# A fused attention and FFN kernel on one core: all 3,359 operations of its hand-kept order put at new places

## The chip, the core and the metric

The kernel runs on one core of one Trainium2 chip. Its engines are TensorE (PE, with PEld for its weight loads), VectorE (DVE), ScalarE (ACT), GpSimd (POOL) and SyncE (SP), and 16 DMA engines move data. The metric is the device time of one launch, in microseconds.

## What is computed

The first half is attention in which a query sees only the keys whose nearest centroid is its own. The second half is a feed-forward layer with the activation h * tanh(softplus(h)), called mish below. The core of the reference:

```python
q_assign = np.argmax(np.einsum('bhsd,hcd->bhsc', q_n, c_n), axis=-1)
k_assign = np.argmax(np.einsum('bhsd,hcd->bhsc', k_n, c_n), axis=-1)
mask = q_assign[:, :, :, None] == k_assign[:, :, None, :]
scores = scale * np.matmul(q, k.transpose(0, 1, 3, 2))
scores = np.where(mask, scores, -1000000000.0)
attn = softmax(scores)                      # over the last axis, with 1e-9 in the divisor
x = np.matmul(attn, v)                      # 4 batches, 8 heads, 768 rows, 64 columns each
h = x.reshape(3072, 512) @ w_in             # 512 x 2048
out = (h * np.tanh(softplus(h))) @ w_out    # 2048 x 512
```

## The kernel before

Attention has 32 groups (batch and head, number n), each with three blocks of 256 queries. Such a block is a unit i, 96 in all, and it has two halves a of 128 queries. For one half the steps are these:

- `scores` (L646, L651): four matmuls fill a tile s in PSUM. Two such tiles exist, and the assignment tiles use the same two.
- `rowmax` (L663, DVE), then `expo` (L677, ACT), which reads s, writes the probabilities p and sets the tile s free. There are three buffers p.
- `total` and `recip` (small DVE operations), `p_hi` (L715, POOL) and `p_lo` (L732, DVE). They split p into a high and a low half-precision part, in a tile hl of which there are three. `p_lo` sets p free.
- `ptrans` (L748): a transposing DMA on SP's queue from hl into the tile pt.
- `pv` (L768): for a pair of units m, 36 matmuls that use 64 of the array's columns each. `pv_out` (ACT) and `x_lo` (DVE) put the result into x.

The first 24 units go another way: transposes on PE (L725), full-precision `pv`. Before a group can be scored its operands A, B, T and Z are made: `prep_hi` and `prep_lo` on POOL, then `copy_t` (T from A), `copy_z`, `copy_b` (B from T), `copy_a` and `hot_copy`, mostly DMAs. Those at L529 are issued by SP or by ACT, and L636 and L637 by SP. `v_load` and `v_sq` bring the values in by SP and square them on ACT (L383).

The feed-forward layer has matmuls `m1` (h, L847 to L849), the activation `e_mish` (L858, ACT), `e_gh` (POOL) and `e_gl` (L872, DVE), and matmuls `m2` (O, L984 to L986). Its result goes out by `m_out` (L992, ACT) and `m_store` (L998, SP). The last part is done with seven block products instead of eight (`n_mul`, `k_mul`).

ACT changes its table between exponential and mish; each change is a row ACT_TABLE_LOAD.

The order of all this is written out: the string `ORDER` has one entry per operation, `RANK` gives its place, and `Plan.run` emits the operations sorted by it. `Plan.tie` makes each engine run its instructions in the order in which they were emitted, and gives the buffers out in that order. So the string sets, for each engine and each DMA queue, what stands behind what.

Of the kernel before, what the change touches and what calls it, by code (L numbers as in the profile page):

```python
# [1568 lines left out]
w_low 1, scores 0 1, rowmax 0 0, rowmax 0 1, w_f32 3, copy_z 1, w_abs 2, hot_copy 1, expo 0 0, expo 0 1, w_abs 0, p_hi
0 1, w_low 0, p_hi 0 0, scores 1 0, p_lo 0 0, scores 1 1, p_lo 0 1, scores 2 0, rowmax 1 0, w_f32 2, v_max 0, rowmax 1  # L1570
1, w_f32 1, w_f32 0, rowmax 2 0, ptrans 0 0, expo 1 0, ptrans 0 1, expo 1 1, p_hi 1 1, p_hi 1 0, p_lo 1 0, scores 2 1,
v_cross 0, p_lo 1 1, ptrans 1 0, copy_b 1, rowmax 2 1, v_peak 0, ptrans 1 1, expo 2 0, w_low 7, prep_hi 2, w_low 6,
prep_lo 2, total 0 1, w_low 17, total 1 1, w_low 5, w_low 4, p_hi 2 0, w_abs 7, expo 2 1, p_hi 2 1, w_sq 0, pv 0 0,
p_lo 2 0, scores 3 0, v_wide 0, scores 3 1, pv 0 1, w_f32 7, recip 0 1, rowmax 3 0, recip 1 1, rowmax 3 1, copy_t 2,
w_load 9, w_load 8, copy_z 2, qk_load 4, hot_copy 2, copy_a 2, w_load 15, copy_b 2, w_load 12, pv 0 2, p_lo 2 1,
scores 4 0, ptrans 2 0, w_abs 5, w_abs 6, w_abs 4, expo 3 0, expo 3 1, ptrans 2 1, p_hi 3 1, p_hi 3 0, p_lo 3 0,
scores 4 1, w_sq 1, p_lo 3 1, scores 5 0, w_f32 6, w_f32 4, v_scale 0, rowmax 4 0, pv_out 0, pv_out 1, rowmax 4 1,
x_lo 0, x_lo 1, ptrans 3 0, expo 4 0, ptrans 3 1, expo 4 1, p_hi 4 1, p_hi 4 0, w_sq 2, p_lo 4 0, w_low 8, w_low 16,
total 3 1, total 4 1, total 2 1, prep_hi 3, prep_lo 3, w_low 9, recip 3 1, rowmax 5 0, recip 4 1, recip 2 1, w_f32 5,
total 1 0, w_abs 8, ptrans 4 0, w_abs 9, expo 5 0, total 0 0, recip 0 0, recip 1 0, scores 5 1, p_lo 4 1, pv 1 0, pv 1  # L1580
1, p_hi 5 0, pv 1 2, w_sq 3, p_lo 5 0, scores 6 0, w_f32 8, rowmax 5 1, ptrans 4 1, w_abs 17, w_f32 17, expo 5 1,
pv_out 2, p_hi 5 1, total 5 1, w_abs 12, recip 5 1, w_abs 16, ptrans 5 0, w_low 12, w_low 10, pv_out 3, w_low 15,
rowmax 6 0, expo 6 0, x_lo 3, scores 6 1, w_sq 4, w_sq 5, w_sq 6, w_sq 7, p_lo 5 1, scores 7 1, w_f32 9, rowmax 6 1,
ptrans 5 1, w_f32 12, rowmax 7 1, expo 6 1, x_lo 2, p_hi 6 1, p_hi 6 0, p_lo 6 0, scores 7 0, pv 2 0, qk_load 5,
qk_load 7, w_load 14, w_load 13, w_load 21, qk_load 6, copy_z 3, copy_t 3, hot_copy 3, w_load 20, copy_b 3, copy_a 3,
w_load 18, w_load 22, w_load 19, v_load 1 0, total 3 0, rowmax 7 0, w_abs 11, w_abs 10, w_abs 14, w_abs 15, w_abs 13,
expo 7 0, ptrans 6 0, expo 7 1, p_hi 7 1, recip 3 0, total 4 0, recip 4 0, total 2 0, recip 2 0, pv 2 1, pv 2 2, w_low
11, w_low 14, w_low 13, total 6 1, total 7 1, w_f32 11, w_f32 14, recip 6 1, w_f32 10, w_f32 13, w_f32 15, w_f32 16,
w_low 21, pv_out 4, p_hi 7 0, assign_mm 1, p_lo 6 1, scores 8 0, w_sq 8, w_sq 9, p_lo 7 0, scores 8 1, w_sq 10, w_sq
11, w_sq 12, p_lo 7 1, w_sq 13, w_sq 14, total 5 0, x_lo 4, assign_turn 1, rowmax 8 0, assign_max 1, recip 7 1, rowmax  # L1590
8 1, ptrans 6 1, w_abs 21, ptrans 7 0, expo 8 0, prep_hi 4, w_f32 21, ptrans 7 1, w_sq 15, expo 8 1, total 8 1, pv_out
5, w_sum 0, p_hi 8 0, p_lo 8 0, scores 9 0, w_spread 0, pv 3 0, p_hi 8 1, assign_hot 1, rowmax 9 0, assign_back 1, pv
3 1, pv 3 2, assign_put 1, scores 9 1, recip 5 0, w_scale 0, recip 8 1, assign_stg 1, rowmax 9 1, w_abs 20, ptrans 8
0, expo 9 0, w_abs 18, pv_out 6, pv_out 7, x_lo 6, x_lo 7, p_hi 9 0, p_lo 8 1, scores 10 0, w_sq 16, p_lo 9 0, ptrans
8 1, expo 9 1, ptrans 9 0, w_low 20, w_low 22, prep_lo 4, w_low 19, w_low 18, w_hi 0, p_hi 9 1, w_f32 18, rowmax 10 0,
w_lo 0, scores 10 1, p_lo 9 1, ptrans 9 1, rowmax 10 1, expo 10 0, expo 10 1, w_abs 19, total 6 0, recip 6 0, w_sq 17,
pv 4 0, total 9 1, w_hi 1, recip 9 1, w_f32 20, w_lo 1, p_hi 10 1, p_hi 10 0, p_lo 10 0, scores 11 0, pv 4 1, pv 4 2,
copy_t 4, copy_a 4, copy_z 4, hot_copy 4, w_load 25, copy_b 4, w_load 26, w_load 23, total 9 0, recip 9 0, scores 11
1, p_lo 10 1, total 10 1, w_hi 2, prep_hi 5, ptrans 10 0, w_abs 22, rowmax 11 0, w_f32 19, recip 10 1, pv_out 8, expo
11 0, pv_out 9, rowmax 11 1, w_lo 2, ptrans 10 1, x_lo 8, x_lo 9, total 7 0, recip 7 0, p_hi 11 0, expo 11 1, p_hi 11  # L1600
1, prep_lo 5, w_hi 3, total 11 1, scores 12 0, w_sq 18, w_sq 19, w_sq 20, p_lo 11 0, scores 12 1, p_lo 11 1, w_sq 21,
scores 13 0, ptrans 11 0, rowmax 12 0, expo 12 0, rowmax 12 1, ptrans 11 1, w_abs 23, expo 12 1, w_abs 26, w_lo 3,
w_f32 22, recip 11 1, rowmax 13 0, total 8 0, recip 8 0, copy_t 5, v_load 1 2, v_load 1 3, copy_z 5, w_load 24,
qk_load 8, copy_b 5, hot_copy 5, copy_a 5, qk_load 9, w_load 29, w_load 27, w_load 28, w_load 30, p_hi 12 1, w_hi 4,
p_hi 12 0, pv 5 0, p_lo 12 0, scores 13 1, p_lo 12 1, pv 5 1, pv 5 2, w_lo 4, rowmax 13 1, ptrans 12 0, w_abs 25, expo
13 0, ptrans 12 1, expo 13 1, w_hi 5, total 12 1, w_lo 5, w_low 23, pv_out 10, w_low 25, recip 12 1, pv_out 11, w_low
26, w_low 24, total 13 1, prep_hi 6, x_lo 11, p_hi 13 0, p_lo 13 0, w_sq 22, scores 14 0, scores 14 1, p_hi 13 1, x_lo
5, total 10 0, recip 10 0, p_lo 13 1, ptrans 13 0, w_f32 23, rowmax 14 0, rowmax 14 1, ptrans 13 1, w_abs 24, expo 14
0, expo 14 1, v_sq 1 0, p_hi 14 0, w_sq 23, pv 6 0, pv 6 1, p_lo 14 0, scores 15 0, scores 15 1, w_hi 6, w_low 27,
prep_lo 6, total 14 1, w_low 28, w_low 30, w_low 29, p_hi 14 1, w_f32 25, w_f32 26, recip 13 1, w_f32 24, rowmax 15 0,  # L1610
rowmax 15 1, w_lo 6, moe_scale_h 0, p_lo 14 1, pv 6 2, total 11 0, recip 11 0, ptrans 14 0, v_sq 1 2, ptrans 14 1,
expo 15 0, pv_out 12, expo 15 1, pv_out 13, p_hi 15 0, w_sq 24, p_lo 15 0, scores 16 0, w_sq 25, ptrans 15 0, w_abs
27, p_hi 15 1, total 12 0, recip 12 0, x_lo 10, x_lo 13, p_lo 15 1, scores 16 1, rowmax 16 0, ptrans 15 1, w_f32 27,
rowmax 16 1, recip 14 1, total 15 1, expo 16 0, w_abs 28, w_abs 29, expo 16 1, p_hi 16 0, pv 7 0, w_sq 26, w_sq 27,
p_lo 16 0, scores 17 0, p_hi 16 1, copy_t 6, copy_z 6, w_load 31, hot_copy 6, copy_a 6, copy_b 6, qk_load 10, v_load 1
1, total 16 1, w_low 31, prep_hi 7, recip 15 1, w_f32 28, w_f32 29, rowmax 17 0, total 15 0, recip 15 0, scores 17 1,
pv 7 1, pv 7 2, w_sq 28, w_sq 29, p_lo 16 1, w_abs 30, ptrans 16 0, expo 17 0, w_abs 31, w_f32 30, rowmax 17 1, w_f32
31, expo 17 1, pv_out 14, ptrans 16 1, total 17 1, pv_out 15, prep_lo 7, w_hi 7, x_lo 15, x_lo 14, p_hi 17 1, p_hi 17
# [295 lines left out]
```

## Time and profile before

| | us |
|---|---|
| three timed runs | 860.67, 857.17, 860.91; median 860.67 |
| the profiled execution | 856.9, of which the span of its instructions 855.2 |
| PE busy | 833.8 (97%) |
| DVE, ACT, POOL busy | 675.7 (79%), 544.1 (64%), 433.6 (51%) |
| DMA | mean 143 GB/s, 122.50 MB |

Busy time counts an engine as busy from an instruction's start to its end; matmuls are pipelined and their ends are modelled. The difference between the span and the execution's time lies before the first and behind the last instruction.

### The profile page before, as it was taken

How to read it: one execution, taken by the hardware profiler on the slowest of the kernel's cores; microseconds unless marked ns; L12 is line 12 of the kernel's file. 1: busy time of each engine (PE TensorE's matmuls, PEld its weight loads, DVE VectorE, ACT ScalarE, POOL GpSimd, SP SyncE). 2: the span in 40 equal slices, each digit the busy share in tenths (PEclk: the TensorE clock that was granted, in tenths of full speed). 3: DMA queues.
4: the chain of work that ended last, by engine and by line, in shares of the span. 5: the costliest groups of instructions: out<-in, count | busy, mean ns of one | idle time of the engine just before them, and what ended most of it. 6: DMA issues, size and time to landing. Idle time of an engine off the chain costs nothing.

```text
span 855.2 us, 17553 instructions
## 1 busy us (share of the span) xinstructions
PE 833.8 (97%) x6743; PEld 622.9 (73%) x6743; DVE 675.7 (79%) x1192; ACT 544.1 (64%) x925; POOL 433.6 (51%) x417
## 2 busy tenths in 40 slices
...
GB/s 339 298 247 185 213 135 43 114 192 163 176 200 154 174 181 122 148 163 116 173 153 174 190 171 127 150 177 162 136 146 146 148 112 96 15 1 2 2 8 80
DMA packets 253460, 122.50 MB, mean 143 GB/s; under 512 B 230368, under 2 KB 230880, under 8 KB 253376
## 3 DMA queue, kind: packets, MB, share of 16 engines
...
## 4 chain that ended last, share of the span: by engine, by line
PE 52%; DVE 4%; DMA 3%; ACT 2%; POOL 1%; issue 1%; ACTq 0%; SPq 0%; POOLq 0%; DVEq 0%
PE h L847 7%; PE h L849 6%; PE h L848 6%; PE o L768 5%; PE O L984 5%; PE O L985 5%; PE O L986 5%; PE s L646 3%; PE s L651 3%; DMA pt<-hl 2%; PE cn L937 2%; DVE hl L732 1%; PE cy('k', 1)_10960 L1131 1%; PE cy('k', 0)_10720 L1131 1%; DVE m L663 1%
## 5 line engine op out<-in xcount | busy, mean ns | idle before, releaser
L677 ACT ACTIVATE p<-s,m 128x768 f32<-128x768 f32 x192 | 173.0, 902 | 120.4 <-DVE m L663 59.1
L715 POOL TENSOR_SCALAR hl<-p,l 128x768 f16<-128x768 f32 x144 | 157.3, 1095 | 168.2 <-DVE l L697 92.5
L663 DVE TENSOR_REDUCE m<-s 128x1 f32<-128x768 f32 x192 | 179.8, 949 | 29.5 <-PE s L651 27.1
L732 DVE SCALAR_TENSOR_TENSOR hl<-p,l,hl 128x768 f16<-128x768 f32 x144 | 165.7, 1159 | 30.2 <-POOL hl L715 30.0
L847 PE MATMUL h<-x,w 128*128 128x256 f16 x640 | 175.2, 274 | 0.0
L849 PE MATMUL h<-x,w 128*128 128x256 f16 x640 | 174.5, 273 | 0.0
L848 PE MATMUL h<-x,w 128*128 128x256 f16 x640 | 174.4, 273 | 0.0
L646 PE MATMUL s<-A,B 128*128 128x384 f32 x384 | 117.0, 385 | 11.8 <-ACT p L677 10.0
L984 PE MATMUL O<-w,g 128*128 128x512 f16 x288 | 109.8, 381 | 0.0
L986 PE MATMUL O<-w,g 128*128 128x512 f16 x288 | 109.2, 379 | 0.0
L985 PE MATMUL O<-w,g 128*128 128x512 f16 x288 | 109.2, 379 | 0.0
L651 PE MATMUL s<-Z,T 80*128 80x384 f32 x384 | 99.2, 339 | 0.4 <-DVE T L618 0.4
L847 PEld LDWEIGHTS <-w 128*128 128x128 f16 x768 | 75.1, 98 | 24.4 <-issue 13.2
L864 POOL TENSOR_SCALAR g<-u,mscg 128x512 f16<-128x512 f32 x72 | 70.8, 987 | 43.5 <-ACT u L858 24.9
L848 PEld LDWEIGHTS <-w 128*128 128x128 f16 x768 | 75.3, 98 | 11.3
L646 PEld LDWEIGHTS s<-A,B 128*128 128x128 f32 x384 | 62.0, 190 | 29.2 <-ACT p L677 17.1
L849 PEld LDWEIGHTS <-w 128*128 128x128 f16 x768 | 75.1, 98 | 8.7
L858 ACT ACTIVATE u<-h,msch 128x512 f32<-128x512 f32 x80 | 53.8, 687 | 43.1 <-PE h L849 28.8
L768 PE MATMUL o<-pt,v 128*64 128x256 f16 x1296 | 78.1, 274 | 0.8 <-DMA pt<-hl 0.8
L768 PEld LDWEIGHTS <-v 128*64 128x64 f16 x1296 | 68.1, 110 | 11.8 <-issue 11.3
L872 DVE SCALAR_TENSOR_TENSOR g<-u,mscg,g 128x512 f16<-128x512 f32 x72 | 69.0, 964 | 5.9 <-POOL g L864 5.8
L651 PEld LDWEIGHTS s<-Z,T 80*128 80x128 f32 x384 | 69.9, 189 | 0.7 <-ACT w L285 0.7
(241 smaller groups left out, 1393.2 us busy)
## 6 DMA issues: line engine op xcount, KB each, us to landing
...
```

Source lines behind the costliest of these rows:

```text
L646: nc.tensor.matmul(s[:, j, :384], st["B", n][:, q0 : q0 + P], st["A", n][:, j * 384 : (j + 1) * 384], start=True, stop=False,)
L651: nc.tensor.matmul(s[:, j, :384], st["T", n][: D + NCL, q0 : q0 + P], st["Z", n][: D + NCL, j * 384 : (j + 1) * 384], start=False, stop=True,)
L663: nc.vector.tensor_reduce(m, st["s", i, a][:, :, :384], axis=AX.XY, op=ALU.max, negate=True)
L677: nc.scalar.activation(p.rearrange("p (n x) -> p n x", n=2), st["s", i, a][:, :, :384], AF.Exp, bias=st["m", i, a], scale=1.0, accum_out=l,)
L715: nc.gpsimd.tensor_scalar(t[:, 0], p, r, 1.0, op0=ALU.mult, op1=ALU.mult)
L732: nc.vector.scalar_tensor_tensor(t[:, 1], p, r, t[:, 0], op0=ALU.mult, op1=ALU.subtract)
L768: nc.tensor.matmul(o[s * D : s * D + D, :256], v if early else v[:, int(part == 1)], st["pt", 2 * m + s][:, :, c + (0 if early or part < 2 ...
L847: nc.tensor.matmul(o, wh, xh, start=(c == 0), stop=False)
L848: nc.tensor.matmul(o, wh, xl, start=False, stop=False)
L849: nc.tensor.matmul(o, wl, xh, start=False, stop=(c == 3))
L984: nc.tensor.matmul(o, gh, wh, start=(f == 0 and fi == 0), stop=False)
L985: nc.tensor.matmul(o, gh, wl, start=False, stop=False)
```

## The change

Every operation keeps its work, its engine and its buffers; only the string `ORDER` is another. The diff replaces all 317 lines of it. Two pairs of lines show what it looks like:

```diff
-21 1, pv 21 2, e_mish 20, e_mish 21, copy_t 16, pv_out 42, pv_out 43, m1 23 0, scores 46 0, m1 23 1, scores 47 0, m2 2
-16, ptrans 45 0, ptrans 45 1, expo 46 1, copy_b 16, copy_a 16, expo 46 0, rowmax 47 0, expo 47 0, copy_t 17, e_mish
...
+16, p_hi 44 0, e_gh 18, expo 45 0, copy_t 16, expo 45 1, m_out 1 1, e_mish 20, assign_put 4, scores 47 0, pv 21 0,
+ptrans 45 0, ptrans 45 1, copy_b 16, expo 47 0, expo 46 1, copy_a 16, expo 46 0, e_mish 22, total 46 1, recip 46 1,
```

Most operations stay within a few places of where they stood. PE has as many matmuls as before. ACT loses four table loads, 96 before and 92 now.

**First place: ACT, the copies of group 16.** This is ACT's order around the middle of the program, with the DMA that copies T from A at the top and the one that copies B from T below it. Names are out<-in, and p46_1 is the tile p of unit 46, half 1. Before:

```order
L529 DMA T_16_4351<-A_16_4243 64x768
L805 ACTIVATE x1_3_0_4353<-o21_4297 64x256
L805 ACTIVATE x1_3_1_4355<-o21_4297 64x256
L677 ACTIVATE p46_1_4465,l46_1_4466<-s46_1_4292,m46_1_4318 128x768
L529 DMA B_16_4246<-T_16_4351 64x768
L527 CAST A_16_4243<-A_16_4243 64x768
L677 ACTIVATE p46_0_4470,l46_0_4471<-s46_0_4370,m46_0_4450 128x768
L677 ACTIVATE p47_0_4475,l47_0_4476<-s47_0_4387,m47_0_4473 128x768
```

ACT's order with the change, from the same copy of T to the first exponential behind the copy of B:

```order
L529 DMA T_16_4270<-A_16_4259 64x768
L677 ACTIVATE p45_1_4272,l45_1_4273<-s45_1_4131,m45_1_4254 128x768
L992 ACTIVATE osb1_1_4275<-O1_1_3951,msco0_2275 128x512
L857 ACT_TABLE_LOAD
L858 ACTIVATE u20_4278<-h20_4193,msch0_1834 128x512
L805 ACTIVATE x1_3_0_4348<-o21_4289 64x256
L805 ACTIVATE x1_3_1_4350<-o21_4289 64x256
L858 ACTIVATE u21_4352<-h21_4230,msch0_1834 128x512
L860 ACT_TABLE_LOAD
L383 ACTIVATE vq2_0_4355,vm2_3782<-vraw2_0_4183 128x768
L529 DMA B_16_4262<-T_16_4270 64x768
L677 ACTIVATE p47_0_4466,l47_0_4467<-s47_0_4284,m47_0_4447 128x768
```

Three operations stood between the two copies, and nine stand there now.

**Second place: ACT, the squares of the last batch's values.** vq3_1 is the square of the tile vraw3_1, which a DMA on SP's queue loads. ACT before, from the copy of B of group 23:

```order
L529 DMA B_23_6402<-T_23_6549 64x768
L858 ACTIVATE u43_6616<-h43_6521,msch1_3891 128x512
L860 ACT_TABLE_LOAD
L383 ACTIVATE vq3_1_6752,vm3_6751<-vraw3_1_6743 128x768
L805 ACTIVATE x2_2_1_6234<-o32_6637 64x256
L805 ACTIVATE x2_2_2_6556<-o32_6637 64x256
L677 ACTIVATE p68_0_6756,l68_0_6757<-s68_0_6516,m68_0_6625 128x768
```

ACT with the change, from the same copy of B:

```order
L529 DMA B_23_6404<-T_23_6555 64x768
L677 ACTIVATE p68_0_6755,l68_0_6756<-s68_0_6512,m68_0_6624 128x768
L805 ACTIVATE x2_2_1_6226<-o32_6640 64x256
L805 ACTIVATE x2_2_2_6557<-o32_6640 64x256
L383 ACTIVATE vq3_0_6761,vm3_6760<-vraw3_0_6593 128x768
L677 ACTIVATE p69_0_6799,l69_0_6800<-s69_0_6689,m69_0_6769 128x768
```

The exponential of unit 68 now stands ahead of the square, and it is another tile's square. Among the rows of SP's queue the load of vraw3_1 moved from 259 to 248, that of vraw3_0 from 241 to 250, that of vraw3_3 from 224 to 245 and that of vraw3_2 from 263 to 269.

**Third place: SP, the store of osb2_0.** This is SP's queue of DMAs; osb2_0 is written by ACT's `m_out`. Before:

```order
L489 DMA qk23_4707<-in_qk_dram 128x768
L636 DMA Z_17_4704<-stg4_4444 16x768
L637 DMA T_17_4478<-stg4_4444 16x768
L748 DMA_TRANSPOSE pt48_4950<-hl48_0_4694 128x12x128
L748 DMA_TRANSPOSE pt48_4950<-hl48_1_4696 128x12x128
L748 DMA_TRANSPOSE pt49_4953<-hl49_1_4904 128x12x128
L998 DMA out_0_dram<-osb2_0_4761 128x512
```

SP with the change, at the same stretch:

```order
L636 DMA Z_17_4679<-stg4_4306 16x768
L637 DMA T_17_4653<-stg4_4306 16x768
L529 DMA A_17_4441<-A_17_4441 64x768
L489 DMA qk23_4684<-in_qk_dram 128x768
L998 DMA out_0_dram<-osb2_0_4775 128x512
L748 DMA_TRANSPOSE pt48_4969<-hl48_1_4671 128x12x128
```

The store stood behind three transposes of units 48 and 49; now it stands ahead of them, and on ACT `m_out` of osb2_0 stands seven rows behind the exponential of unit 48, half 1.

## Rows read from the trace of the kernel before

**Rows 1.** The page: the span, and PE's and other engines' busy time.

```profile
span 855.2 us, 17553 instructions
...
PE 833.8 (97%) x6743; PEld 622.9 (73%) x6743; DVE 675.7 (79%) x1192; ACT 544.1 (64%) x925; POOL 433.6 (51%) x417
```

**Rows 2.** Busy time by stretch: its length, each engine's busy us, clock, DMA.

```profile
20.00:200.00 180.00, 173.67 (x1426) 135.53 (x1428) 164.05 (x275) 143.32 (x295) 127.51 (x132) 0.99 0.72 181
200.00:700.00 500.00, 491.69 (x3935) 355.23 (x3932) 396.47 (x688) 323.67 (x506) 287.12 (x259) 1.00 0.83 156
700.00:840.00 140.00, 140.00 (x1207) 115.06 (x1206) 96.05 (x184) 61.54 (x99) 14.92 (x16) 1.00 0.12 26
```

**Rows 3.** PE's groups in 200 to 700 us: count, busy, mean ns, idle before.

```profile
L646 PE MATMUL s<-A,B 128*128 128x384 f32 x252 | 77.7, 389 | 6.5 <-ACT p L677 5.6 <-issue 0.9
```

**Rows 4.** Timeline at 310 to 321 us, ACT and PE: start, length, idle before.

```profile
310.79 0.47 ACTq L529 DMA_DIRECT2D T<-A  x1
317.84 0.47 ACTq L529 DMA_DIRECT2D B<-T  x1
318.35 0.83 ACT L527 CAST A<-A 64x768 fp32r<-64x768 f32 x1 [3.69 <-issue]
320.25 0.62 PE L646 MATMUL s<-A,B 128*128 128x384 f32 x2 [0.90 <-ACT p L677]
```

**Rows 5.** Timeline at 486 to 497 us, SP, ACT and PE.

```profile
486.83 1.78 SPq L371 DMA_DIRECT2D vraw<-in_vP_dram  x1
493.65 0.84 ACT L383 ACTIVATE vq<-vraw 128x768 bf16<-128x768 f32 x1 [3.25 <-DMA vraw<-in_vP_dram]
496.44 0.61 PE L646 MATMUL s<-A,B 128*128 128x384 f32 x2 [1.20 <-ACT p L677]
```

**Rows 6.** Timeline at 350 to 353 us, ACT and PE.

```profile
350.31 1.28 ACT L677 ACT_TABLE_LOAD   x1 [1.37 <-DVE hl L732]
351.60 0.90 ACT L677 ACTIVATE p<-s,m 128x768 f32<-128x768 f32 x1
352.65 0.61 PE L646 MATMUL s<-A,B 128*128 128x384 f32 x2 [0.71 <-ACT p L677]
```

**Rows 7.** Timeline at 652 to 661 us, SP and PE.

```profile
652.34 1.44 SPq L748 DMA_TRANSPOSE pt<-hl  x1
656.37 0.59 SPq L529 DMA_DIRECT2D A<-A  x1
660.33 0.58 PE L646 MATMUL s<-A,B 128*128 128x384 f32 x2 [0.86 <-issue]
```

**Rows 8.** Timeline at 324 to 327 us, PE: a `pv` between two kinds.

```profile
324.04 0.52 PE L651 MATMUL s<-Z,T 80*128 80x384 f32 x2
324.49 2.16 PE L768 MATMUL o<-pt,v 128*64 128x256 f16 x36
326.58 0.39 PE L984 MATMUL O<-w,g 128*128 128x512 f16 x1
```

**Rows 9.** PE at 31 us and at 137 to 142 us, and the clock there.

```profile
30.91 1.95 PE L768 MATMUL o<-pt,vraw 128*64 128x256 f32 x16
137.16 0.62 PE L646 MATMUL s<-A,B 128*128 128x384 f32 x2 [1.55 <-ACT p L677]
138.16 3.51 PE L768 MATMUL o<-pt,vraw 128*64 128x256 f32 x16
138.00:140.00 2.00, 2.00 (x12) 1.17 (x12) 2.00 (x3) 0.00 (x0) 0.55 (x1) 0.59 0.04 6
```

**Rows 10.** Groups over the whole span: count, busy us, mean ns, idle.

```profile
L677 ACT ACTIVATE p<-s,m 128x768 f32<-128x768 f32 x192 | 173.0, 902 | 120.4 <-DVE m L663 59.1 <-DVE hl L732 25.7 <-DVE l L689 12.5
L992 ACT ACTIVATE osb<-O,msco 128x512 f32<-128x512 f32 x18 | 12.4, 686 | 15.9 <-PE O L986 15.7
L732 DVE SCALAR_TENSOR_TENSOR hl<-p,l,hl 128x768 f16<-128x768 f32 x144 | 165.7, 1159 | 30.2 <-POOL hl L715 30.0
L715 POOL TENSOR_SCALAR hl<-p,l 128x768 f16<-128x768 f32 x144 | 157.3, 1095 | 168.2 <-DVE l L697 92.5 <-DMA pt<-hl 33.2 <-issue 11.8
```

**Rows 11.** DMA issues: count, median us from issue to landing.

```profile
pt<-hl SPq DMA_TRANSPOSE x144, 4.1
```

More of the change, by code (lines that the diff above doesn't have):

```diff
@@ L1569 @@
[L1569 to L1618, printed above, removed]
@@ L1769 @@
-m1 44 0, m1 44 1, scores 70 0, m_out 4 1, copy_t 24, v_sq 3 2, expo 69 1, pv_out 66, pv_out 67, copy_a 24, e_mish 44,
-v_sq 3 0, p_lo 69 0, e_gl 42, total 69 1, x_lo 66, x_lo 67, p_lo 68 1, p_lo 68 0, e_gl 43, rowmax 70 0, recip 69 1, m1
-45 1, scores 70 1, m2 5 0 0, m1 47 0, scores 71 0, assign_put 6, m2 5 0 1, m2 5 0 2, m1 47 1, scores 71 1, e_gh 44,
-p_hi 69 1, rowmax 70 1, p_lo 69 1, rowmax 71 0, moe_scale_h 2, assign_stg 6, ptrans 69 0, copy_z 24, m_store 4 1,
-ptrans 68 1, ptrans 68 0, ptrans 69 1, hot_copy 24, expo 70 0, copy_b 24, expo 70 1, expo 71 0, v_sq 3 3, e_mish 45,
@@ new lines @@
+15 0, w_abs 27, rowmax 16 0, w_f32 27, rowmax 16 1, ptrans 15 1, recip 15 1, recip 14 1, w_abs 30, expo 16 0, w_abs
+29, expo 16 1, w_abs 28, p_hi 16 0, pv 7 0, w_sq 26, w_sq 27, p_lo 16 0, scores 17 0, scores 17 1, pv 7 1, p_hi 16 1,
+copy_t 6, copy_z 6, hot_copy 6, w_load 31, copy_b 6, copy_a 6, qk_load 11, v_load 1 3, w_low 30, w_low 28, prep_hi 7,
+w_low 29, w_low 31, w_f32 30, rowmax 17 0, rowmax 17 1, w_f32 28, w_f32 29, total 15 0, recip 15 0, pv 7 2, w_sq 28,
+p_lo 16 1, ptrans 16 0, expo 17 0, expo 17 1, w_abs 31, w_f32 31, pv_out 14, ptrans 16 1, total 16 1, total 17 1,
@@ new lines @@
+prep_lo 7, pv_out 15, w_hi 7, x_lo 15, x_lo 14, p_hi 17 1, p_hi 17 0, w_sq 29, w_sq 30, w_sq 31, w_sum 1, p_lo 17 0,
+scores 18 0, ptrans 17 0, total 13 0, recip 13 0, p_lo 17 1, scores 18 1, rowmax 18 0, recip 16 1, recip 17 1, ptrans
+17 1, expo 18 0, pv 8 0, w_spread 1, rowmax 18 1, w_scale 1, w_lo 7, p_hi 18 0, p_lo 18 0, expo 18 1, ptrans 18 0,
+p_hi 18 1, scores 19 0, scores 19 1, p_lo 18 1, pv 8 1, w_hi 8, total 18 1, rowmax 19 0, rowmax 19 1, w_lo 8, pv 8 2,
+v_sq 1 3, ptrans 18 1, expo 19 0, expo 19 1, copy_z 7, copy_t 7, qk_load 10, v_load 1 1, hot_copy 7, copy_b 7, copy_a
@@ new lines @@
+ptrans 39 0, pv_out 36, pv_out 37, expo 41 0, expo 40 1, expo 40 0, v_sq 2 1, copy_b 14, copy_a 14, x_lo 36, total 41
+0, x_lo 37, total 40 0, total 40 1, recip 40 0, recip 41 0, e_gl 15, recip 40 1, v_split 1 3, rowmax 41 1, m1 17 1, m2
+1 0 4, m2 1 0 5, m1 16 1, m2 1 0 6, m2 1 0 7, scores 42 1, pv 19 0, prep_hi 15, prep_lo 15, p_hi 41 0, p_hi 40 0, p_hi
+40 1, copy_t 15, v_sq 2 3, e_mish 16, e_mish 17, m_out 1 0, expo 41 1, copy_a 15, p_lo 41 0, p_lo 40 1, rowmax 42 1,
+moe_scale_h 1, total 41 1, recip 41 1, p_lo 40 0, pv 19 1, pv 19 2, m1 19 0, scores 43 0, scores 43 1, m2 1 1 0, m2 1
@@ new lines @@
+scores 53 0, m1 28 0, m1 28 1, e_mish 26, e_mish 27, expo 52 0, m_out 2 1, copy_a 18, copy_b 18, pv_out 48, pv_out 49,
+expo 52 1, e_gh 26, p_hi 51 1, p_hi 51 0, p_lo 51 1, total 52 0, p_lo 51 0, recip 52 0, e_gl 26, rowmax 53 1, rowmax
+53 0, ptrans 50 0, hot_copy 18, ptrans 50 1, ptrans 51 0, ptrans 51 1, expo 53 1, e_mish 28, expo 53 0, m1 30 0, m1 30
+1, scores 54 0, scores 54 1, pv 25 0, pv 25 1, pv 25 2, m1 29 0, m1 31 0, p_hi 52 0, e_gh 27, prep_hi 19, copy_t 19,
+e_mish 30, x_lo 48, p_lo 52 0, total 52 1, recip 52 1, total 53 1, x_lo 49, e_gl 27, moe_scale_o 1, rowmax 54 0, recip
@@ new lines @@
+hot_copy 24, expo 70 0, copy_a 24, expo 70 1, e_mish 45, copy_b 24, expo 71 0, v_sq 3 2, e_gl 44, total 70 0, total 70
+1, recip 70 0, e_gh 45, prep_hi 25, p_hi 70 0, e_gl 45, rowmax 71 1, total 71 0, recip 71 0, v_max 3, p_lo 70 0, recip
+70 1, m2 5 0 3, m1 47 1, pv 34 0, pv 34 1, pv 34 2, m1 46 0, m1 46 1, m2 5 0 4, scores 72 1, scores 72 0, copy_t 25,
+pv_out 68, pv_out 69, expo 71 1, e_mish 46, e_mish 47, prep_lo 25, p_hi 71 0, p_hi 70 1, e_gh 47, e_gh 46, x_lo 69,
+x_lo 68, total 71 1, moe_scale_h 2, p_lo 70 1, recip 71 1, p_lo 71 0, rowmax 72 1, rowmax 72 0, e_gl 47, e_gl 46, m1
```

548 lines of the change are left out of this document (289 added, 259 removed).

## The prediction

> **What bounds the kernel now.** I read the page first: PE is busy for 833.8 of 855.2 us [rows 1], so a change that keeps all matmuls can only work on the 21.4 us in which PE stands idle, and on slow stretches inside the busy time. The table of stretches comes next [rows 2]. From 700 to 840 us PE is busy for 140.00 of 140.00: nothing is to be had there. From 20 to 200 us PE lacks 180.00 - 173.67 = 6.3 us, and DVE is busy for 164.05 of 180.00, that is 91%. PE's waits there are those for an engine that is nearly full, and another order gives DVE no less work. From 200 to 700 us PE lacks 500.00 - 491.69 = 8.3 us while DVE stands at 79% and ACT at 65%, so those waits come from places, not from load. The groups of PE in that stage say which: 6.5 of the 8.3 us stand before the first matmul of a `scores`, 5.6 of them put down to ACT's `expo`, which sets the tile s free, and 0.9 to nothing the profile names [rows 3].
>
> I then looked at single waits. At 320.25 PE stands 0.90 us [rows 4]. The reader is to see ACT: its `copy_b` was issued at 317.84 and the work behind it began after 3.69 us of idle, because `copy_b` reads the T that ACT's own DMA at 310.79 still had to bring. Behind it stood the two exponentials that PE needed. At 496.44 PE stands 1.20 us [rows 5]: ACT had waited 3.25 us at a `v_sq` for a load that SP had issued at 486.83, with the next exponential behind it. At 352.65 it is 0.71 us [rows 6]: an exponential with a table load of 1.28 us ahead of it. At 660.33 it is 0.86 us [rows 7], and no engine is named: the first `scores` of group 30 needs `copy_a`, which SP issued at 656.37, behind a transpose at 652.34 that had held the queue.
>
> **The change, part by part.** The written order decides what I can count: what stands between what, on each engine.
>
> The first place: between `copy_t` and `copy_b` of group 16 ACT had two `pv_out` and an `expo`, and now has nine operations with two table loads, over 5 us of rows in all. The transfer took up to 317.84 - 310.79 = 7.1 us [rows 4], so the new spacing covers most of it, and the exponentials no longer stand directly behind. I take the whole 0.90 us (bounds 0 and -0.90). In the other 20 groups whose two copies ACT issues, two more had so short a spacing (10 and 25), and none has it now; they show no wait of PE that I can tie to them, so I add nothing.
>
> The second place: three of the last batch's four loads stand at rows 245, 248 and 250 of SP's queue, where the load that was waited for stood at 259, and the `expo` of unit 68 stands ahead of the first square. I take the 1.20 us (bounds 0 and -1.20).
>
> At 352.65 the `expo` of unit 50, half 0, had its own table load; in the new order it directly follows that of half 1, and the load comes behind both. The 1.28 us is more than the wait, so I take 0.71. Three other loads are gone elsewhere; ACT stands idle 35% of the stage [rows 2], and I count them at nothing (if each stood on a wait, 3 x 1.28 = 3.8 us, a bound).
>
> At 660.33 a `pv` and an `m2` of six matmuls now stand right ahead of the first scores of group 30: 2.1 us and 6 x 0.22 = 1.3 us of work [rows 8], 3.4 us more cover. But on SP three transposes instead of one stand ahead of `hot_copy`; two more of 1.44 us [rows 7] take 2.9 us of it. I take half, 0.4 us (bounds 0 and -0.86).
>
> Of the 5.6 us by `expo`, 5.6 - 0.90 - 1.20 - 0.71 = 2.8 us are left. An `expo` also needs a free p. Counting DVE's order, `p_lo` of three halves before stands behind the `rowmax` of the same half in 68 of 141 cases before and in 59 now, and the DVE work by which it is behind sums to 194 and 160 us at mean row lengths. I take the same 18% off: -0.5 us (bounds 0 and -2.8).
>
> Matmuls that change the number of array columns cost a little. The third and fourth of `scores` start at 324.04 and about 0.18 later; the `pv` starts 0.27 behind that, 0.09 more than usual, and the O behind it again some 0.09 late [rows 8]. The new order has 124 such changes and the old one 127: 3 x 0.09 = -0.3 us.
>
> In 20 to 200 us one place costs more than its wait: after 1.55 us of idle at 137.16, sixteen matmuls take 3.51 us which took 1.95 at 30.91, and the granted clock of 138 to 140 us is 0.59, that is partly at the lower level of 1.2 GHz [rows 9]. The same DVE operations precede the exponential in question as before, but `rowmax` of unit 21 now stands behind the transpose of the assignment. PE's wait should fall into two shorter ones. If the clock then stays, 1.56 us is saved; I take half, -0.8. The other 6.3 us I leave (bounds -2 and +2: one wait of the size of [rows 9] more or less).
>
> The third place can cost. The store of osb2_0 stands ahead of the transpose of hl48_1. From the end of that half's `expo`, ACT has three more exponentials (0.90 each), two table loads (1.28 each), one mish and `m_out` (0.69 each) before SP may go on: 6.6 us [rows 6, 10]. By itself the half would be ready after `p_hi` and `p_lo`, 1.10 + 1.16 = 2.3 us [rows 10]. So the transpose issues 4.4 us late. It matters to POOL, which takes the same hl again three halves later: 6.6 + 4.1 us to landing [rows 11] = 10.7 us, against 3 x 4.0 = 11.9 us at the mean spacing of 126 halves in 500 us (252 matmuls, two a half [rows 3]). At mean spacing it just fits; halves in quick succession would lose up to 4.4. I take +0.5 (bounds 0 and +4.4).
>
> **The sum**, against the profiled execution: 856.9 - 0.9 - 1.2 - 0.7 - 0.4 - 0.5 - 0.3 - 0.8 + 0.5 = 852.6. The median of the three runs, 860.67, is 3.8 above the profiled one. The same 4.3 us off it give 856.4.
>
> On ACT the four loads that are gone are 4 x 1.28 = 5.1 us by the rows, and the exponential starts as the load ends (350.31 + 1.28, 351.60 [rows 6]). The Trainium skill (ScalarE: Activation LUTs, "What ACT_TABLE_LOAD costs") puts 1283 ns for the load, which agrees, and a drain of 1380 ns with it, which this trace does not show. By the page ACT would have 10.6 us less, and if the three loads outside the sum all stood on waits, the sum would lose up to 8.0 us more; by the rows it is 3.8 at most, and the sum stays.
>
> **Rivals.** First, the waits move: each order gives PE eight or so waits of about 1 us in these 500 us, and the new one has them at other places. For it: the spread of causes (a DMA, a load, a table, a queue). Against it: the counts above all go one way. It gives 856.9 - 0.3 = 856.6 profiled, 860.4 on the median.
>
> Second, slower: SP's queue becomes the wait. A store, or copies that wait for a landing, ahead of transposes hold hl, then POOL, `p_lo`, p, `expo` and PE. It decides once halves around unit 48 come closer than 10.7 us for three. Then 4.4 us are lost there, and a PE wait of that length is followed by the lower clock as in [rows 9], another 1.6: +6.0, and with the waits merely moved elsewhere 860.7 + 6.0 - 0.3 = 866.4. Against it: of the stores that have over 5 us of ACT work between the half behind them and their own input, the old order had five and the new one has two.
>
> Third, that the change does not do what its title says: drains are 0.3 us, so by that part alone the time stays, 860.4, the same as the first rival.
>
> **Chances.** My forecast 0.58, waits that move 0.29, SP's queue 0.13. Measurement tells about 0.5%, or 4.3 us, from no change; my forecast lies on that edge, and three of the things that it counts at nothing (the loads, two short copy spacings, the 6.3 us) are more likely gains than losses. Of its 0.58 I put 0.44 beyond 4.3 us, of the first rival 0.03; faster has 0.47. Slower has 0.11 of the second rival and 0.03 of the others, 0.14. The same 0.39. The range: with all bounds taken at their best (-0.9 - 1.2 - 0.7 - 0.9 - 2.8 - 0.3 - 1.6 - 2, and a load or two) 12 us come off, 848.5; upward it takes in most of the second rival, 865. The forecast's own range is 850 to 860.
>
> **What would show it.** Right: in 200 to 700 us PE lacks 4 to 6 us in place of 8.3; no ACT idle of over 2 us before the work behind a `copy_b`; no wait of ACT for vraw above 1 us; at about 137 us two waits under 1 us and a clock of 1.00. Wrong: a wait of SP for osb around 340 us with POOL idle for pt behind it; the first `scores` of group 30 still late; new waits at `m1` 24, which now stands 3.4 us of PE's work behind the `pv` it needs, where 8.7 us lay between. The forecast falls if DVE's 91% before 200 us gives PE other waits, or if the waits left are as many as before.

## The result, and the profile after

The changed kernel takes 849.97 us (median of six runs, 848.06 to 851.86), the kernel before beside it 859.84 (six runs, 855.67 to 860.91). The ratio is 0.9892, with a 95% interval of 0.9865 to 0.9919: 1.1% faster; the medians differ by 9.9 us. Measured a second time (after_2, below), the same kernel stood at 0.988 (0.9845 to 0.9916) of before. The time lies in the range of the prediction, near its low end; the forecast of 4.3 us was less than half of the gain. The profiled execution took 850.43 us.

The page after: busy time of the engines, which answers to [rows 1].

```profile
span 848.7 us, 17556 instructions
...
PE 832.1 (98%) x6742; PEld 624.3 (74%) x6743; DVE 674.8 (80%) x1192; ACT 539.4 (64%) x921; POOL 423.2 (50%) x417
```

The stretches after, with the columns of [rows 2]:

```profile
0.00:20.00 20.00, 15.41 (x67) 6.28 (x68) 13.72 (x37) 13.76 (x23) 3.21 (x11) 1.00 0.92 334
20.00:200.00 180.00, 172.82 (x1425) 134.91 (x1424) 159.89 (x276) 139.60 (x292) 120.02 (x131) 1.00 0.72 179
200.00:700.00 500.00, 498.42 (x3988) 361.88 (x3985) 404.89 (x696) 328.40 (x514) 286.12 (x262) 1.00 0.83 159
700.00:840.00 140.00, 140.00 (x1224) 116.63 (x1222) 95.38 (x183) 57.13 (x91) 13.15 (x16) 1.00 0.11 27
```

And the first stretch of the kernel before, in the same view:

```profile
0.00:20.00 20.00, 16.43 (x73) 6.61 (x73) 15.19 (x38) 14.57 (x26) 3.34 (x11) 1.00 0.92 334
```

The reader is to see three things. From 200 to 700 us PE now lacks 1.6 us where it lacked 8.3: -6.7. In the first 200 us it lacks 4.6 + 7.2 us where it lacked 3.6 + 6.3: +1.9, a loss. And PE's busy time is 1.7 us less for the same matmuls. Together 6.5 us, the difference of the two spans. The medians differ by 9.9; the rest is mostly in the kernel before, whose profiled run (856.9) lay 2.9 us under its median, while that of after lies 0.5 above. The experiments come back to it.

The clock did not fall at 140 us. PE's group that ran at the lower clock there in [rows 9] is busy 2.0 us less, before and then after:

```profile
L768 PE MATMUL o<-pt,vraw 128*64 128x256 f32 x288 | 37.6, 399 | 0.0
```

```profile
L768 PE MATMUL o<-pt,vraw 128*64 128x256 f32 x288 | 35.6, 386 | 0.1
```

PE's group in 200 to 700 us, which answers to [rows 3]; the 6.5 us of idle time are 0.8:

```profile
L646 PE MATMUL s<-A,B 128*128 128x384 f32 x250 | 78.3, 394 | 0.8 <-ACT p L677 0.8
```

The first place: ACT's copies of group 16 in the timeline after [rows 4 for before].

```profile
306.87 0.47 ACTq L529 DMA_DIRECT2D T<-A  x1
...
315.32 0.48 ACTq L529 DMA_DIRECT2D B<-T  x1
315.57 1.28 ACT L860 ACT_TABLE_LOAD   x1
```

8.45 us lie between the copies, and ACT goes on 0.25 us behind the second one's issue. At the squares of the last batch one wait for a load is left, of 1.33 us at 515.22, with no wait of PE behind it. The third place, SP's queue after:

```profile
342.36 1.51 SPq L998 DMA_DIRECT2D out_dram<-osb  x1
343.99 3.40 SPq L748 DMA_TRANSPOSE pt<-hl  x1
```

The transpose of hl48_1 goes out at 343.99. Its `p_lo` ran from 340.84 to 341.86 on DVE, so it is 2.1 us late and not 4.4, and between 288 and 567 us PE has no wait above 0.2 us. What was lost stands at the start, on PE and ACT:

```profile
8.11 0.94 ACT L496 ACTIVATE A<-qk,scq 128x768 fp32r<-128x768 f32 x1 [0.31 <-DMA qk<-in_qk_dram]
10.06 0.84 ACT L383 ACTIVATE vq<-vraw 128x768 bf16<-128x768 f32 x1 [1.01 <-DMA vraw<-in_vP_dram]
16.79 0.59 ACT L615 ACTIVATE Z<-put 16x512 fp32r<-16x512 f32 x1
...
18.31 0.59 PE L651 MATMUL s<-Z,T 80*128 80x384 f32 x2 [1.34 <-DVE T L618]
19.36 0.59 PE L646 MATMUL s<-A,B 128*128 128x384 f32 x2 [0.46 <-DVE vsm L414]
```

ACT writes the one-hot rows into Z (L615) at 16.79 where it did so at 15.22 before. The same work stands ahead of it, but ACT now waits 0.31 and 1.01 us for loads: on SP the load of group 1 stands third and no longer first, and the four value loads follow one another where weights stood between them. `scores` of the first unit goes on at 18.31 for 16.74.

### The profile page after: what moved, and what is told of

The parts are those of the page before. It is cut to its first block, busy times and chain, and to the rows that moved or that the text cites. A ratio compares the mean times of both kernels' runs of the same rounds, so it can differ in the third digit from the quotient of the medians.

```text
span 848.7 us, 17556 instructions
## 1 busy us (share of the span) xinstructions
PE 832.1 (98%) x6742; PEld 624.3 (74%) x6743; DVE 674.8 (80%) x1192; ACT 539.4 (64%) x921; POOL 423.2 (50%) x417
## 4 chain that ended last, share of the span: by engine, by line
PE 70%; DVE 13%; POOL 5%; ACT 4%; DMA 4%; issue 3%; SPq 0%; ACTq 0%; POOLq 0%; DVEq 0%
PE o L768 8%; PE h L847 8%; PE h L849 8%; PE h L848 8%; PE O L984 6%; PE O L986 6%; PE O L985 6%; PE s L646 5%; PE s L651 5%; DVE hl L732 4%; DVE m L663 3%; PE cn L937 2%; ACT p L677 2%; DMA pt<-hl 2%; DMA qk<-in_qk_dram 1%
## 5 line engine op out<-in xcount | busy, mean ns | idle before, releaser
L677 ACT ACTIVATE p<-s,m 128x768 f32<-128x768 f32 x192 | 172.8, 901 | 131.9 <-DVE m L663 69.7
L715 POOL TENSOR_SCALAR hl<-p,l 128x768 f16<-128x768 f32 x144 | 154.4, 1075 | 169.4 <-DVE l L697 86.2
L663 DVE TENSOR_REDUCE m<-s 128x1 f32<-128x768 f32 x192 | 180.2, 950 | 49.0 <-PE s L651 46.7
L732 DVE SCALAR_TENSOR_TENSOR hl<-p,l,hl 128x768 f16<-128x768 f32 x144 | 173.1, 1214 | 24.5 <-POOL hl L715 23.7
L864 POOL TENSOR_SCALAR g<-u,mscg 128x512 f16<-128x512 f32 x72 | 62.3, 871 | 45.7 <-ACT u L858 42.3
L872 DVE SCALAR_TENSOR_TENSOR g<-u,mscg,g 128x512 f16<-128x512 f32 x72 | 64.6, 902 | 2.6 <-POOL g L864 2.5
```

The source lines that it names most:

```text
L663: nc.vector.tensor_reduce(m, st["s", i, a][:, :, :384], axis=AX.XY, op=ALU.max, negate=True)
L677: nc.scalar.activation(p.rearrange("p (n x) -> p n x", n=2), st["s", i, a][:, :, :384], AF.Exp, bias=st["m", i, a], scale=1.0, accum_out=l,)
L732: nc.vector.scalar_tensor_tensor(t[:, 1], p, r, t[:, 0], op0=ALU.mult, op1=ALU.subtract)
```

## Experiments

All times are compared with the kernel before on the same chip.

### Which part of the order makes the gain: x_head, x_mid

```diff
# x_head
-ORDER: 3,359 entries of the old string
+ORDER: the first 1,021 entries of the new string, the other 2,338 in the old string's order
# x_mid
-ORDER: 3,359 entries of the old string
+ORDER: the first 1,021 entries of the old string, the other 2,338 in the new string's order
```

> The first 1,021 operations stand in the new order (they end at about 190 us), the other 2,338 in the old one. By the theory that each wait of PE belongs to a place in the order, the waits of before in 200 to 700 us are all there (PE lacks about 8.3 us), those of after before 200 us too (PE lacks 11.8 us in 0 to 200 where before lacks 9.9), and the clock stays at 1.00 at 140 us, which is worth some 2 us: together the time of before within 1 us. By the rival that waits only move, the stage from 200 to 700 us has waits at other places than before. If the whole gain came from the head, this kernel would be 6 to 10 us faster than before.

> The first 1,021 operations stand in the old order, the other 2,338 in the new one. Places theory: PE lacks 1.6 us in 200 to 700 us as in after, in 0 to 200 us 9.9 us as in before, and the slow stretch of the clock at 138 to 140 us is there again: 6 to 7 us faster than before. Rival, waits move: the start comes at other times than in after, so the middle gets waits again, 4 us or more, and the gain is under 4 us.

x_head: 1.0019 (0.9993 to 1.0045), not told apart from before, though its clock stays at 1.00 as expected. x_mid: 0.9881 (0.9848 to 0.9914), 1.2% faster, and by the medians 8.5 us (847.79 against 856.33), more than the 6 to 7 expected. Their stretches, x_head and then x_mid:

```profile
200.00:700.00 500.00, 489.61 (x3899) 352.76 (x3899) 399.72 (x685) 321.74 (x505) 285.75 (x257) 1.00 0.83 156
```

```profile
200.00:700.00 500.00, 498.51 (x3993) 362.78 (x3990) 401.71 (x695) 325.63 (x512) 282.29 (x261) 1.00 0.82 158
```

The whole gain is in what stands behind operation 1,021 (about 190 us). The new middle keeps its 1.5 us of idle time although it begins at another time and behind another head, so its gain is not the luck of one alignment. The old middle lacks 10.4 us behind the new head, 2.1 more than in [rows 2]; the longest wait that came in is one of 1.19 us at 304 us, which the profile of before does not have.

### The loads of ACT's table: b_load

```diff
-        if j % 2 and j < 72:
+        if j < 72 and (j % 2 or NEXT[j] == "expo"):
             nc.scalar.preload_act_table_set("natural_log_exp_and_others")
...
+_act = [op for op in sorted(RANK, key=RANK.get) if op[0] in ("e_mish", "expo")]
+NEXT = {a[1]: b[0] for a, b in zip(_act, _act[1:]) if a[0] == "e_mish"}
```

> The order of before; only the loads of the exponential's table that stood directly at an exponential (11 of them, between two mish activations of one pair) are written out right behind the mish activation, so that they do not start with the exponential's own wait. Theory, the load on the path: in before five of the eleven start only when the exponential's input is there, after 0.8 to 3.4 us of idle, and PE waits 0.71, 1.09 and 0.84 us behind those at 350, 381 and 511 us and 0.30 us behind that at 183 us. These four waits go: PE lacks 5.7 us in 200 to 700 us in place of 8.3, and the time is 2.6 to 2.9 us less. Rival, the reading of the prediction: only 0.71 us at 350 us is the load's, the other waits come from the order of DVE's work: about 0.7 us less. Rival, waits move: no change.

The timeline of ACT before, at the two waits of PE at 383 and 513 us that the prediction had put to DVE's order:

```profile
380.69 1.28 ACT L677 ACT_TABLE_LOAD   x1 [2.20 <-DVE hl L732]
381.99 0.90 ACT L677 ACTIVATE p<-s,m 128x768 f32<-128x768 f32 x1
...
510.71 1.28 ACT L677 ACT_TABLE_LOAD   x1 [0.79 <-DVE l L697]
```

The same two places in b_load:

```profile
378.46 1.28 ACT L860 ACT_TABLE_LOAD   x1
380.68 0.90 ACT L677 ACTIVATE p<-s,m 128x768 f32<-128x768 f32 x1 [0.94 <-DVE hl L732]
...
508.25 1.28 ACT L860 ACT_TABLE_LOAD   x1
```

A load that stands at its exponential (line L677) waits for the exponential's input and then takes its 1.28 us on the path. One that is written out (L860) starts 0.02 us behind the instruction ahead of it and runs inside that wait. All four waits of PE are gone as the theory said: at none of the places is more than 0.15 us left. PE lacks 7.0 us in the middle, 2.36 of it at 304 us, where the profile of before has no wait. The time is 0.9985 (0.9958 to 1.0013): the expected 2.6 to 2.9 us are inside the interval, but the times do not show them, and the medians (857.32 against 856.33) lie the other way.

### The old order's other places: b_dma, b_swap, b_total

```diff
# b_dma
 expo 45 0,
+copy_t 16,
...
-copy_t 16, pv_out 42, pv_out 43,
+pv_out 42, pv_out 43,
...
-v_sq 3 1, pv_out 64, pv_out 65, expo 68 0,
+pv_out 64, pv_out 65, expo 68 0, v_sq 3 1,
...
-scores 90 0, m2 7 0 3, m2 7 0 4,
+m2 7 0 3, m2 7 0 4, scores 90 0,
# b_swap
-rowmax 21 1, assign_back 2,
+assign_back 2, rowmax 21 1,
# b_total
-w_lo 9, expo 21 1, pv_out 18, total 20 1, pv_out 19,
+total 20 1, w_lo 9, expo 21 1, pv_out 18, pv_out 19,
```

> The order of before with three moves: the copy of T of group 16 stands ahead of a square, an exponential and two mish activations where it stood behind them; the square of vraw3_1 stands behind the exponential of unit 68, half 0; two of the m2 of block 7 (12 matmuls, 2.6 us) stand ahead of the first scores of group 30. Theory, each term of the prediction has its place: the waits of PE at 320 us (0.90), 496 us (1.20) and 660 us (0.86) are gone and the others of 200 to 700 us stay, so PE lacks 5.3 us there in place of 8.3, and the time is 3.0 us less. Rival, waits move: PE finds as much to wait for behind these places, and the time stays within 1 us.

> The order of before with one swap: on VectorE the rowmax of unit 21, half 1, stands behind the transpose of the assignment (0.98 us) and no longer ahead of it. The prediction's reason for the gain at 137 us was this swap: then the wait of 1.55 us at 137 us becomes two under 1 us, the sixteen matmuls behind it take 1.95 us and not 3.51, and 1.6 to 2.2 us are saved. Rival: the wait comes from what stands ahead of the exponential of unit 22 (the weight's sum L365 of 1.24 us and two adds into xf ahead of its rowmax), which the swap leaves: the wait stays over 1 us and the clock falls again.

> The order of before with one operation moved: the sum of unit 20 (L689, two columns) on VectorE stands ahead of the weight's sum L365 and no longer between two adds into xf. In before it took 1.03 us at 133.56, ending with POOL's L359, where others take 0.16; in after it stands ahead of L359 and takes 0.16. Theory, contention: this one operation is the cause of 0.87 of the 1.55 us at 137 us; the wait becomes 0.7 us, and the rest of the kernel stays: 0.9 us less, and 1.6 more in those executions that had the slower clock behind the wait. Rival: the wait has its length from the rest of the chain, and stays at 1.2 us or more as with the swap.

b_dma: 1.0002 (0.9977 to 1.0026), no gain. The wait at 320 us is gone and that at 496 us is 0.47 us; but PE lacks 8.6 us in the middle, where it lacked 8.3. The next two kernels, whose middle has the order of before, lack 8.8 and 9.0 us: the three moves took off 0.2 to 0.4 us and not 3.0. At 660 us the two `m2` only brought PE to the next `pv` before its transposes had landed (timeline of PE in b_dma):

```profile
304.01 1.01 PE L646 MATMUL s<-A,B 128*128 128x384 f32 x2 [2.67 <-DVE D L569]
...
664.75 0.30 PE L768 MATMUL o<-pt,v 128*64 128x256 f16 x1 [0.88 <-DMA pt<-hl]
665.76 1.50 PE L768 MATMUL o<-pt,v 128*64 128x256 f16 x24 [0.71 <-DMA pt<-hl]
```

Before had 0.86 us ahead of those `scores` [rows 7] and 0.44 ahead of that `pv`; now it is 0.88 and 0.71 ahead of the `pv`. For that place the rival of waits that move holds.

b_swap: the wait at 137 us is 1.25 us, so the swap that the prediction named accounts for 0.3 us of it at most (0.9971, 0.9942 to 1.0). Most of it is one small operation. VectorE and POOL before:

```profile
133.56 1.03 DVE L689 TENSOR_SCALAR l<-l 128x2 f32<-128x2 f32 x1
...
133.45 1.12 POOL L359 TENSOR_SCALAR w<-w,ws1r 128x1024 f16<-128x1024 f32 x1
```

and VectorE and PE in b_total, where it stands ahead of POOL's operation:

```profile
132.03 0.12 DVE L689 TENSOR_SCALAR l<-l 128x2 f32<-128x2 f32 x1
...
136.24 0.61 PE L646 MATMUL s<-A,B 128*128 128x384 f32 x2 [0.67 <-ACT p L677]
```

Two columns took 1.03 us and ended at 134.59, with POOL's L359 at 134.57; alone they take 0.12. The wait fell from 1.55 to 0.67 us, as the contention theory said. The Trainium skill (SBUF — State Buffer, "SBUF: two separate sides") says that GpSimd and some operations of VectorE (those in a two-port mode, or with two inputs in SBUF against a GpSimd operation that reads SBUF) share a pair of ports under an exclusive lock, and that whichever comes second stands until the first is done; the two ends 0.02 us apart agree with it, but no run shows in which mode the sum ran. The time (0.9987, 0.9961 to 1.0013) is not told apart from before, with 2.73 us at 304 us again.

### Is the first profile of before typical: before_2

> The kernel before itself, profiled a second time. Its first profile has no wait of PE at 304 us and one of 0.90 us at 320 us; five experiments with the same order there, or nearly, had 1.1 to 2.7 us at 303 to 305 us, and three of them none at 320 us. Theory, edges: the old order stands at an edge there (a transposed tile lands earlier or later by 2 us, and VectorE's e_gl, 0.74 us long elsewhere, takes 2.3 us when it falls on a POOL subtraction), so this profile shows 2.3 to 2.7 us at about 304 us, and the first profile was on the lucky side by 1.5 us. Rival: the first profile is what this order does, and the experiments' own edits made the wait: no wait at 304 us and 0.9 at 320 us again.

No edit. The time is 0.9997 (0.9964 to 1.0029), but the profile is another: span 858.8, and its middle stretch is

```profile
200.00:700.00 500.00, 488.34 (x3887) 352.13 (x3882) 394.46 (x686) 321.37 (x503) 283.51 (x256) 1.00 0.84 155
```

11.7 us without PE, 3.4 more than in [rows 2]. PE's waits in that stretch, with total, count and longest:

```profile
PE s L646 <- ACT p L677: 6.5, 7, 2.0
PE s L646 <- DVE D L569: 2.3, 1, 2.3
```

The chain to the second row, in the timelines of POOL, DVE and PE of before_2:

```profile
298.76 0.91 POOL L715 TENSOR_SCALAR hl<-p,l 128x768 f16<-128x768 f32 x1 [4.46 <-DMA pt<-hl]
...
302.13 2.39 POOL L515 TENSOR_TENSOR B<-qk,A 128x768 fp32r<-128x768 f32 x1
...
302.77 2.30 DVE L872 SCALAR_TENSOR_TENSOR g<-u,mscg,g 128x512 f16<-128x512 f32 x1
305.10 0.98 DVE L569 STREAM_TRANSPOSE D<-as 128x768 f32<-128x768 f32 x1
...
306.14 0.61 PE L646 MATMUL s<-A,B 128*128 128x384 f32 x2 [2.32 <-DVE D L569]
```

and in the first profile of before:

```profile
296.28 0.91 POOL L715 TENSOR_SCALAR hl<-p,l 128x768 f16<-128x768 f32 x1 [2.28 <-DMA pt<-hl]
...
299.75 1.30 DVE L872 SCALAR_TENSOR_TENSOR g<-u,mscg,g 128x512 f16<-128x512 f32 x1
301.08 0.98 DVE L569 STREAM_TRANSPOSE D<-as 128x768 f32<-128x768 f32 x1
```

The transposed tile came 2.2 us later (4.46 for 2.28 us of waiting); POOL's subtraction (L515) then began ahead of VectorE's `e_gl` (L872), which took 2.30 us for 1.30, and the transpose of the assignment, which frees the tile s, began 4.0 us later on the clock of the trace, 0.3 of which it had brought along. b_load, b_dma, b_swap and b_total, with the same order there, have this wait at 304 or 305 us, 2.36 to 2.73 us long. None of these four has the wait at 320 us, though b_dma alone had moved the copy; before_2 has 0.67 us left of it, and x_head has both (1.19 and 1.28). For the wait at 304 us the first profile of before was the exception.

In the sum of the middle the first profile lies at one end and before_2 at the other: b_swap and b_total, whose edits stand ahead of 150 us, lack 8.8 and 9.0 us there, x_head 10.4. Part of the spread of the times goes with the clock: of the 23 executions of before beside before_2, the six with a granted clock of 1.00 have a mean span of 854.5 us, the eight with 0.998 one of 857.6.

### All single repairs together: b_all

```diff
 the edits of b_dma, b_swap and b_load, and
-m1 20 1, e_gl 16, assign_turn 4,
+m1 20 1, assign_turn 4, e_gl 16,
```

> The order of before with all single repairs together: the three moves of the copy, the square and the m2; the swap of the rowmax of unit 21; the eleven loads written out behind the mish activation; and on VectorE the transpose of the assignment 4 ahead of e_gl 16 (0.75 to 2.30 us), behind which a wait of 1.2 to 2.4 us at 304 us came and went between kernels with the same order there. Theory, places add up: 0.90 + 1.20 + 0.86 + 2.6 + 0.3 + 1.6 or more is 7.5 us less than before's profile, PE lacks 2.5 to 3.5 us in 200 to 700 us, and the spread of the runs is smaller than before's. Rival, waits move: under 3 us.

0.9959 (0.9937 to 0.998): by the ratio 3.5 us faster, by the medians (853.89 against 859.01) 5.1, where 7.5 were expected and the new order brings 9.9. PE lacks 5.3 us in the middle. The waits at 320, 353, 383 and 496 us are gone, but PE now stands at others:

```profile
198.27 1.94 PE L768 MATMUL o<-pt,v 128*64 128x256 f16 x32 [1.83 <-DMA pt<-hl]
...
302.63 0.58 PE L646 MATMUL s<-A,B 128*128 128x384 f32 x2 [1.11 <-DVE D L569]
...
310.75 0.62 PE L646 MATMUL s<-A,B 128*128 128x384 f32 x2 [0.89 <-ACT p L677]
```

Single places do not add up: neither theory holds whole. The four waits went, that at 304 us only shrank (1.11), as did that at 137 us (1.25), and part of the time came back at the next tight place.

### SP's queue at a larger dose: a_sp

```diff
 expo 49 1, expo 49 0,
-m_out 2 0,
...
 expo 50 1, expo 50 0,
+m_out 2 0,
```

> The new order with one move: ACT's m_out of osb2_0 stands behind the two exponentials of unit 50, so that the store of osb2_0 on SP, and the transposes of hl48_1, hl49_0 and hl48_0 behind it, are issued some 8 to 9 us later than in after (344 us there). The rival of the prediction, SP's queue blocked, at a larger dose: POOL gets hl back at about 357 us and not at 350, p_lo, the p tiles and the exponentials of units 51 and 52 follow, and PE waits 3 to 6 us, with the slower clock behind it up to 8. Against it, slack: the tiles hl, p and s cover it, and PE waits under 1 us.

0.9981 (0.996 to 1.0003) of before, that is 0.9% or 7.6 us slower than after by the two ratios (0.9981 - 0.9892). One wait makes most of it, and PE works at the lower clock behind it:

```profile
350.51 0.58 PE L984 MATMUL O<-w,g 128*128 128x512 f16 x1 [5.40 <-ACT osb L992]
```

```profile
352.00:354.00 2.00, 2.00 (x8) 1.01 (x7) 0.00 (x0) 0.00 (x0) 0.00 (x0) 0.50 1.15 213
```

The size was foreseen, its way was not: PE stands for the tile O that `m_out` reads, and not for `scores` behind SP's queue. POOL did wait 4.21 us for a transposed hl, from 350.51 to 354.72, but behind PE's wait, while PE was at work. In this run a late `m_out` is dear through its PSUM tile first; what SP's queue alone would cost stays open.

### The old start with the new order, and the next wait: x_start, after_2, x_best

```diff
# x_start
-ORDER: 3,359 entries of the new string
+ORDER: the first 77 entries of the old string, the other 3,282 in the new string's order
# x_best: x_start, the edit of b_load, and
-prep_lo 10, p_hi 26 0,
+p_hi 26 0, prep_lo 10,
```

> The first 77 operations stand in the old order (up to about 21 us), the rest in the new one. Theory: the new start costs 1.5 us (the second matmuls of scores begin at 19.36 us in place of 17.79, since ACT takes up the first group's two copies and the last of the consts' squares ahead of what PE waits for), and nothing behind it gives that back: 1.5 us faster than after, 848.5 where after has 850. Rival: VectorE, busy for 89% of 20 to 200 us, is the bound there, and what is gained at the start is lost at its next waits: the time of after.

> The changed kernel itself again, beside the next one on the same chip. Theory, the order's slack: the same short list of waits as in its first profile (1.3 at 18 us, 1.2 at 176 us, 0.5 at 287 us, all others under 0.7), 1.6 us without PE in 200 to 700 us, times of 848 to 852 us, and a spread of a third of before's. Rival, luck of one profile: waits of 1 to 2.5 us at other places, as the kernels with the old order show them.

> The start of before (77 operations), the new order behind it, the table loads written out behind the mish activation, and on POOL p_hi of unit 26, half 0, ahead of prep_lo of group 10 (2.12 us). In after and in the kernel with the old start PE waits 1.2 us at 172 to 176 us for an exponential that has waited for p_lo of that half, which waited for this p_hi. Theory: that wait goes, 1.0 to 1.2 us; the written-out loads bring nothing, since no wait of PE stands behind one in this order; with the start 2.5 to 2.9 us less than after. Rival: prep_lo 2 us later, or VectorE, which is busy for 92% there, makes PE wait for as much at the next scores, and only the 1.5 us of the start are left.

x_start: 0.9867 (0.9834 to 0.99), span 844.7. Scores of the first unit go on at 17.07 and 18.12, 1.2 us ahead of after, and the span is 4.0 us shorter: PE lacks 1.2 us less in the first 20 us and 1.7 less from 20 to 200, and is busy for 1.5 us less. after_2 (no edit) lacks 1.5 us in 200 to 700 us with its longest wait there 0.47 us, and has the wait of 1.21 us at 175.8 us again. Not as expected, it has a wait of 1.00 us at 47.7 us and the clock at 0.50 behind the waits of the start, and its times spread over 4.8 us (before's 23 over 10.7). x_best: 0.9861 (0.9822 to 0.9901), span 845.6. Its wait at 172 us is

```profile
171.94 0.62 PE L646 MATMUL s<-A,B 128*128 128x384 f32 x2 [0.69 <-ACT p L677]
```

0.69 us for 1.21, since `p_lo` of that half, now earlier, fell on POOL's subtraction and took 2.01 us; and a `pv` waits 1.26 us for its transposes at 196 us. So the rival holds there. The three intervals overlap: the old start shortens the span, but that either version beats the changed kernel is not shown by the times.

## Why the prediction came out as it did

**The account it started from.** The sum was made against 856.9 us and the 8.3 us that PE lacked in that execution, and the new kernel's profile was taken to lie as far under its median as before's. That is the main step that failed: a single profile was taken for what the order does. Of five profiles whose middle has the order of before, 8.3 us is the lowest and the 11.7 of before_2 the highest. The new order lacks 1.5 to 1.9 us in all four profiles that hold its middle without an edit to it (after, after_2, x_mid, x_start). So the middle gained 6.7 us against the first profile and 7.2 to 10.1 against the other four. Of the 9.9 us between the medians, 3.4 are the distances of the two profiles from them (2.9 + 0.5), and no term of the sum held these. That the time lies in the range all the same is in part luck: its low end took every bound at its best.

**The waits taken singly.** The 0.90 us at 320 us, the 1.20 at 496, the 0.71 at 353 and the 0.86 at 660 are gone, each at its place; the first and the last were sized too unsurely to be terms: the first is gone in b_load, b_swap and b_total too, whose order there is that of before, with a longer one at 304 us, and the other moves to the next `pv` when it is repaired alone. The square's wait goes from 0.91 us in b_swap to 1.96 in before_2.

**The remaining 2.8 us, priced at -0.5.** This is the term of the sum that was mis-sized: its three waits (1.09 us at 383, 0.84 at 513, 0.87 at 581) all went, and with two that came in (0.28 and 0.48) it measured -2.0. It was put to the order of DVE, by a count of `p_lo` behind `rowmax`. b_load shows that a table load completes the waits at 383 and 513 us: it started only when the exponential's input was there, at 381 us behind a `p_lo` (L732), so that the prediction had half of that one. Five of the eleven loads at an exponential waited for its input in before; one of nine does so after, and PE has no wait behind it. These two loads are not among those that the change takes away. It has them at the same exponentials (units 54 and 70, half 0), where the input is there in time:

```profile
380.02 1.28 ACT L677 ACT_TABLE_LOAD   x1
...
505.42 1.28 ACT L677 ACT_TABLE_LOAD   x1
```

So the bound of 3.8 us for loads that are gone has nothing to do with them. The third wait is missing in b_load, b_dma, b_swap and b_total too, which left its place alone; its going is not shown to be the change's.

**The clock at 137 us, priced at -0.8.** The wait of 1.55 us is 0.35 at 140 us after, and the clock stays at 1.00, which is worth the 2.0 us of the group shown above. The reason given was wrong (b_swap); the sum of unit 20 behind POOL's operation made 0.88 us of the wait (b_total). The order alone does not decide on the clock: behind the same wait it stays up in b_load and b_dma, and in after_2 it falls at 20 us.

**The 6.3 us before 200 us, left at 0.** They became 7.2, and the first 20 us lost 1.0 (0.2 between before_2 and after_2): the prediction did not go into the first rows of the order.

**The third place, +0.5.** It cost nothing: the transpose was 2.1 us late. The rival priced at 866.4 did not come; a_sp shows such a loss at 8 us more of delay, and through another tile. **The column changes, -0.3,** were not measured apart.

**The signs it named.** PE lacks less than the 4 to 6 us named for the middle, one wait of ACT for vraw stayed above 1 us (1.33), and ACT stands 2.40 us behind the `copy_b` at 341.97, though there for a result of PE; the wait and the clock at 137 us came as named. Of those of being wrong none came as a wait of PE in the middle: none at `m1` 24, none before the first `scores` of group 30.

**The rival that waits move** is refuted for the new order as a whole (x_mid, after_2) and holds for single repairs of the old one (b_dma, b_all). What stays open is which of the thousands of moves behind operation 1,021 give the new middle its slack; it was shown only that the six repairs of b_all do not.
